# Each store of 128 finished tokens issued as two stores of 64 rows, one per batch (delta rule and gated feed-forward, one core)

## The chip, the core and the metric

The kernel runs on one core of one Trainium2 chip. The core has a matmul engine (TensorE; PE in the profile, its weight loads PEld), VectorE (DVE), ScalarE (ACT), GpSimd (POOL) and SyncE (SP), which here issues every transfer between memory (HBM) and the on-chip buffer (SBUF); the transfers themselves run on 16 DMA engines. The metric is the device time of one execution in microseconds (us), shorter being better. The kernel before took 704.14 us, the median of three runs (702.71 to 704.75).

## The reference

Two stages follow each other. The first is a delta rule over 768 time steps for 4 batches of 8 heads with head size 48; in each step the state of a head is read by the query and then corrected by the key:

```python
k_n = k / (np.linalg.norm(k, axis=-1, keepdims=True) + 1e-06)
for t in range(S):
    y[:, :, t] = np.einsum('bhd,bhde->bhe', q[:, :, t], state)
    v_old = np.einsum('bhde,bhd->bhe', state, kt)
    state = state + bt[:, :, :, None] * np.einsum('bhd,bhe->bhde', kt, vt - v_old)
```

The second is a feed-forward block on the 4 x 768 = 3072 tokens of 384 features that come out: `h = x @ w_in` (384 to 2048), `g = h * tanh(log1p(exp(h)))`, and `g @ w_out` (2048 to 384). The result has 3072 rows of 384 float32, ordered by batch and then by time.

## The kernel before, in words

Time is cut into 12 chunks of 64 steps. One unit `n` handles chunk `n` of all four batches, that is 256 tokens. The chunk form of the delta rule needs the products of a chunk's keys, transposed keys (`kt`, line 264) and a small triangular inverse that is built by a chain of VectorE instructions (`early`, lines 330 to 339); this is done for two chunks at a time, well ahead of their use. The keys for it come in by `load_src` (lines 176 to 183) into the buffers `ksrc`: eight loads per chunk, each of 32 rows, all issued by SyncE through `load` (line 171). The second set of eight follows in the same buffer once the first set has been transposed. Other loads of a unit bring queries (`qsrc`), keys (`xx`) and values (`vt`).

The feed-forward of a unit goes through 8 pairs of feature blocks: `g1` (line 561 on) makes `h` by 18 matmuls of line 575 and applies the nonlinearity on ScalarE and VectorE (lines 588 to 595); `g2` (line 600 on) adds to the two accumulators `acc[0]` and `acc[1]` by 12 matmuls of line 610. Each accumulator holds 128 tokens. Matmuls of the next units' delta rule are woven in between. After the last pair, `store(t)` copies accumulator `t` into an SBUF tile `o` with ScalarE (line 616) and SyncE issues the transfer to the output (line 618). There are 24 of these transfers: two for each of the 12 units. The two accumulators of the last unit are the last work of the kernel; behind them come only SyncE's wait for the transfers and the closing barrier (shown as line 815).

The 128 tokens of one accumulator are 64 time steps of batch `t` and the same 64 steps of batch `t + 2`. In the output these are two stretches of 64 consecutive rows, 1536 rows apart, so the target of line 618 is an access pattern of three dimensions: 2 batches, 64 rows, 384 features. Its source is the tile's 128 partitions with 384 features each.

The order on the engines: the generators put their steps at planned times into one heap (`put`, `defer`), which gives the order of the program; TensorE keeps that order from a planned time of 90 us on, while a scheduler that models the engines orders the instructions of the other engines, SyncE's transfers among them, as their inputs and buffers come free in its model. The order of the loads among themselves is held by line 173; the stores are not part of it. Each queue then runs strictly in order: a transfer whose wait is not over holds back what is behind it.

Of the kernel before, what the change touches and what calls it, by code (L numbers as in the profile page):

```python
# [35 lines left out]
def kernel(  # L36
# [22 lines left out]
    nc = tc.nc  # L59
# [18 lines left out]
    C = 64  # L78
# [37 lines left out]
    def tensor(dur):  # L116

        now[0] = max(now[0], tensor_free[0] if now[0] > TN['clk'] else 0.0)
        tensor_free[0] = now[0] + dur

    def defer(wait, f, *a):
        put(one(f, *a), now[0] + wait)
# [432 lines left out]
    def moe(n):  # L555

        NTT = UT // P
        acc = []
        gs = {}

        def g1(fp):
            end = n == NS - 1
            if end and fp % 3 in TN.get('hx', (2,)):
                h = pa.tile([P, 2, UT], F32, tag="at", name=f"h{n}_{fp}")
            else:
                h = ph.tile([P, 2, UT], F32, tag="h", name=f"h{n}_{fp}")
            xh, xl = xs[n]
            tensor(2.15)
            for f2 in range(2):
                f = 2 * fp + f2  # L570
                i = 0
                for c in range(NCH):
                    f0 = f * P % WI
                    for i2, x in ((0, xh), (0, xl), (1, xh)):
                        nc.tensor.matmul(h[:, f2, :], wt["i", f * P // WI * NCH + c][:, i2, f0:f0 + P], x[:, c, :],  # L575
                                         start=(i == 0), stop=(i == 3 * NCH - 1))
                        i += 1
            e = mp.tile([P, 2, UT], F32, tag="e", name=f"e{n}_{fp}")
            if end:

                gg = ap.tile([P, 2, 2, UT], F32R, tag="tn" if fp % 4 == 3 else "kt", name=f"g{n}_{fp}",
                             bufs=1 if fp % 4 == 3 else 3)
            else:
                gg = mp.tile([P, 2, 2, UT], F32R, tag="g", name=f"g{n}_{fp}", bufs=3)

            eng = nc.gpsimd if n in TN['pg'] else nc.vector
            t = 2.4
            for d, f in ((0.7, lambda: nc.scalar.activation(e, h, AF.Exp, scale=-1.0)),  # L588
                         (0.55, lambda: nc.vector.tensor_scalar(e, e, EXP20, 1.0, op0=ALU.min, op1=ALU.add)),  # L589
                         (0.65, lambda: nc.scalar.activation(e, e, AF.Square)),  # L590
                         (0.65, lambda: nc.scalar.activation(e, e, AF.Ln, bias=0.5, scale=0.5)),  # L591
                         (0.7, lambda: nc.scalar.activation(e, e, AF.Exp, scale=-1.0)),  # L592
                         (0.8, lambda: nc.vector.scalar_tensor_tensor(e, e, -1.0, h, op0=ALU.add, op1=ALU.mult)),  # L593
                         (0.7, lambda: nc.scalar.copy(out=gg[:, 0], in_=e)),  # L594
                         (0.8, lambda: eng.tensor_tensor(out=gg[:, 1], in0=e, in1=gg[:, 0], op=ALU.subtract))):  # L595
                defer(t, f)
                t += d
            gs[fp] = gg

        def g2(fp):  # L600
            gg = gs.pop(fp)
            tensor(2.1)
            if fp == 0:
                acc.extend(po.tile([P, 512], F32, tag=f"acc{t}", name=f"acc{t}_{n}")[:, :DM] for t in range(NTT))
            for t in range(NTT):
                ts_ = slice(t * P, (t + 1) * P)
                for f2 in range(2):
                    f = 2 * fp + f2
                    for i, (a, i2) in enumerate(((0, 0), (0, 1), (1, 0))):
                        nc.tensor.matmul(acc[t], gg[:, a, f2, ts_], wt["o", f][:, i2, :],  # L610
                                         start=(f == 0 and i == 0), stop=(f == NF - 1 and i == 2))

            if fp == NFP - 1:
                def store(t):
                    o = mp.tile([P, 512], F32, tag="w", name=f"o{n}_{t}")[:, :DM]
                    nc.scalar.mul(out=o, in_=acc[t], mul=-1.0)
                    dst = out.rearrange("(hh b r) f -> b hh r f", hh=2, b=2)[t, :, C * n:C * n + C, :]
                    nc.sync.dma_start(out=dst, in_=o)

                for t in range(NTT):  # L620
                    defer(1.3 * (t + 1), store, t)

        return g1, g2
# [196 lines left out]
```

## Time and profile before

| | us |
|---|---|
| median of 3 runs | 704.14 |
| the profiled execution, whole | 702.13 |
| its span, from the first to the last instruction | 700.3 |
| TensorE busy | 633.6 |
| VectorE busy | 478.4 |
| ScalarE busy | 440.0 |
| GpSimd busy | 48.8 |

The profiled execution is 2.0 us shorter than the median, and 1.8 us of it lie outside the span. The last matmul ends at 689.4 us, the last ScalarE instruction at 689.9 us and the span at 700.3 us. TensorE is busy for 90% of the span as a whole; it is below that mainly in the first quarter, where the weights are loaded and converted, and in a few places up to 242 us. The granted clock of TensorE over the span is 0.944 of full speed on average.

### The profile page before, as it was taken

What the parts mean: (1) busy time and instruction counts of PE and PEld (TensorE: products, weight loads), DVE (VectorE), ACT (ScalarE), POOL (GpSimd) and SP (SyncE); (2) the same over time, 40 slices, a digit from 0 to 9 for tenths busy, and PEclk for the clock granted to TensorE, in tenths of its full rate; (3) what the DMA queues carried; (4) which work ended last, traced back from release to release, by engine and by line L of the source; (5) the groups of instructions that cost most, each with busy time, mean ns of one, the idle gap of its engine ahead of it and who ended that gap; (6) DMA issues with size and microseconds to landing.
All of it is one profiled execution on the core that took longest, in us unless ns stands there. A gap on an engine that the chain in (4) does not pass through costs nothing.

```text
span 700.3 us, 23223 instructions
## 1 busy us (share of the span) xinstructions
PE 633.6 (90%) x10163; PEld 582.5 (83%) x10163; DVE 478.4 (68%) x1048; ACT 440.0 (63%) x821; POOL 48.8 (7%) x84
## 2 busy tenths in 40 slices
PE   6543899889979899999999999999999999999993
PEld 3313777679879799999999999999999999999993
DVE  4794278996449975589974799856899645443440
ACT  1350368776535766856758766668566687777771
POOL 5000000101000001010010000010100100000000
PEclk9575589999989999999999999999999999999998
DMA  5999230113131232222212312321121111000000
GB/s 81 223 244 348 40 61 12 22 15 59 27 63 26 42 59 39 41 52 35 46 37 42 63 25 39 66 37 30 31 35 47 28 21 36 13 22 3 12 12 24
DMA packets 160214, 37.79 MB, mean 54 GB/s; under 512 B 153456, under 2 KB 156528, under 8 KB 160112
## 3 DMA queue, kind: packets, MB, share of 16 engines
q1 hardware_dynamic: 160112, 36.30, 25.4%
q8 instruction: 80, 1.31, 0.7%
q14 instruction: 22, 0.18, 0.1%
HBM read 31.56 MB, written 4.72 MB: 52 GB/s over the span
## 4 chain that ended last, share of the span: by engine, by line
PE 44%; DVE 26%; ACT 13%; SPq 7%; issue 6%; DMA 3%; DVEq 0%; ACTq 0%
PE h L575 15%; PE acc L610 15%; SPq L171 7%; DVE e L593 4%; PE gq L433 3%; ACT e L591 3%; DVE g L595 3%; DVE pr L336 3%; DVE gt L338 3%; ACT e L590 2%; PE py L433 2%; ACT e L592 2%; DVE e L589 2%; DVE xx L480 2%; DVE xx L421 2%
## 5 line engine op out<-in xcount | busy, mean ns | idle before, releaser
L575 PE MATMUL h<-x,wi 128*128 128x256 f32 x1728 | 227.0, 285 | 4.3 <-DVE e L593 3.6
L575 PEld LDWEIGHTS h<-x,wi 128*128 128x128 f32 x1728 | 214.4, 188 | 10.5 <-DVE e L593 2.9
L610 PE MATMUL acc<-wo,g 128*128 128x384 f32 x1152 | 221.1, 341 | 0.0
L610 PEld LDWEIGHTS acc<-wo,g 128*128 128x128 f32 x1152 | 198.4, 188 | 3.2
L593 DVE SCALAR_TENSOR_TENSOR e<-e,h 128x512 f32<-128x512 f32 x96 | 65.8, 685 | 97.1 <-ACT e L592 93.8
L590 ACT ACTIVATE e<-e 128x512 f32<-128x512 f32 x96 | 60.6, 631 | 74.6 <-DVE e L589 74.1
L594 ACT CAST g<-e 128x512 fp32r<-128x512 f32 x96 | 59.5, 619 | 41.3 <-DVE e L593 40.8
L595 DVE TENSOR_TENSOR g<-e,g 128x512 fp32r<-128x512 f32 x96 | 65.1, 678 | 20.6 <-ACT g L594 19.4
L588 ACT ACTIVATE e<-h 128x512 f32<-128x512 f32 x96 | 57.1, 595 | 28.5 <-PE h L575 27.6
L591 ACT ACTIVATE e<-e 128x512 f32<-128x512 f32 x96 | 60.5, 631 | 2.6
L592 ACT ACTIVATE e<-e 128x512 f32<-128x512 f32 x96 | 60.6, 632 | 2.4
L589 DVE TENSOR_SCALAR e<-e 128x512 f32<-128x512 f32 x96 | 40.8, 425 | 25.1 <-ACT e L588 24.8
L338 DVE TENSOR_TENSOR gt<-gt,pr 128x84 f32<-128x84 f32 (+14 forms) x148 | 46.0, 311 | 3.2
L336 DVE TENSOR_TENSOR pr<-gt 128x84 f32<-128x84 f32 (+14 forms) x148 | 45.9, 310 | 2.5
L433 PE MATMUL gq<-xx,kt 64*64 64x112 f32 (+1 forms) x768 | 44.6, 264 | 0.9 <-ACT wo L243 0.9
L433 PEld LDWEIGHTS py<-xx 128*64 128x64 f32 x768 | 38.8, 142 | 6.3 <-issue 3.2
L480 DVE TENSOR_TENSOR xx<-gq,amask 64x256 f32<-64x256 f32 x96 | 40.2, 418 | 5.4 <-PE gq L433 4.7
L433 PE MATMUL py<-xx 128*64 128x48 f32 x768 | 42.8, 229 | 0.0
L433 PEld LDWEIGHTS gq<-xx,kt 64*64 64x64 f32 x768 | 38.2, 140 | 2.6 <-issue 1.3
L414 POOL TENSOR_TENSOR vt<-vt,ne 128x384 f32<-128x384 f32 x24 | 21.0, 880 | 277.8 <-DVE ne L328 123.3
L433 PE MATMUL pz<-vt,tt 64*64 64x48 f32 x768 | 38.0, 235 | 2.4 <-ACT tt L462 1.3
L433 PEld LDWEIGHTS pz<-vt,tt 64*64 64x64 f32 x768 | 34.4, 139 | 6.3 <-ACT tt L462 2.8
(112 smaller groups left out, 718.0 us busy)
## 6 DMA issues: line engine op xcount, KB each, us to landing
ri<-in_moe_w_in_dram SPq DMA_DIRECT2D x12, 512.0 KB
ro<-in_moe_w_out_dram SPq DMA_DIRECT2D x16, 384.0 KB
vt<-in_v_dram SPq DMA_DIRECT2D x48, 96.0 KB
xx<-in_k_dram SPq DMA_DIRECT2D x48, 96.0 KB
out_dram<-o SPq DMA_DIRECT2D x24, 192.0 KB
qsrc<-in_q_dram SPq DMA_DIRECT2D x48, 64.0 KB
ksrc<-in_k_dram SPq DMA_DIRECT2D x44, 64.0 KB
qsrc<-in_q_dram SPq DMA_DIRECT2D x48, 32.0 KB
```

What stands on the lines that cost most here:

```text
L336: nc.vector.tensor_tensor(out=pv, in0=nj, in1=xj, op=ALU.mult)
L338: nc.vector.tensor_tensor(out=below, in0=below, in1=pv, op=ALU.add)
L433: last[:] = [nc.tensor.matmul(*a, start=True, stop=True)]
L575: nc.tensor.matmul(h[:, f2, :], wt["i", f * P // WI * NCH + c][:, i2, f0:f0 + P], x[:, c, :], start=(i == 0), stop=(i == 3 * NCH - 1))
L588: for d, f in ((0.7, lambda: nc.scalar.activation(e, h, AF.Exp, scale=-1.0)), (0.55, lambda: nc.vector.tensor_scalar(e, e, EXP20, 1.0, op0 ...
L590: (0.65, lambda: nc.scalar.activation(e, e, AF.Square)),
L591: (0.65, lambda: nc.scalar.activation(e, e, AF.Ln, bias=0.5, scale=0.5)),
L592: (0.7, lambda: nc.scalar.activation(e, e, AF.Exp, scale=-1.0)),
L593: (0.8, lambda: nc.vector.scalar_tensor_tensor(e, e, -1.0, h, op0=ALU.add, op1=ALU.mult)),
L594: (0.7, lambda: nc.scalar.copy(out=gg[:, 0], in_=e)),
L595: (0.8, lambda: eng.tensor_tensor(out=gg[:, 1], in0=e, in1=gg[:, 0], op=ALU.subtract))):
L610: nc.tensor.matmul(acc[t], gg[:, a, f2, ts_], wt["o", f][:, i2, :], start=(f == 0 and i == 0), stop=(f == NF - 1 and i == 2))
```

## The change

Line 618 becomes a loop over the two batches of the accumulator. Each pass issues one transfer: 64 partitions of `o` to the 64 consecutive rows of that batch in the output. The bytes, the copy on ScalarE and the planned time of `store` are as before; SyncE issues 48 transfers to the output in place of 24.

```diff
                     nc.scalar.mul(out=o, in_=acc[t], mul=-1.0)
                     dst = out.rearrange("(hh b r) f -> b hh r f", hh=2, b=2)[t, :, C * n:C * n + C, :]
-                    nc.sync.dma_start(out=dst, in_=o)
+                    for hh in range(2):
+                        nc.sync.dma_start(out=dst[hh], in_=o[C * hh:C * hh + C])
```

## Rows read from the trace of the kernel before

**Rows 1.** The page, busy time of each engine over the span.
```profile
PE 633.6 (90%) x10163; PEld 582.5 (83%) x10163; DVE 478.4 (68%) x1048; ACT 440.0 (63%) x821; POOL 48.8 (7%) x84
```

**Rows 2.** Waits of TensorE from 242 us on: total, times, longest.
```profile
PE h L575 <- DVE e L593: 1.8, 4, 0.5
PE pz L433 <- ACT tt L462: 0.6, 3, 0.2
```

**Rows 3.** Chain of waits, 640 to 701 us: start, length, what.
```profile
681.00 8.39 PE acc L610 x48
...
689.41 0.49 ACT o L616
```

**Rows 4.** Timeline of SyncE's queue, last 13 us: start, length, what.
```profile
689.93 0.51 SPq L618 DMA_DIRECT2D out_dram<-o  x1
...
688.87 1.57 SPq L618 DMA_DIRECT2D out_dram<-o  x2
```

**Rows 5.** Waits of SyncE's queue in the last 13 us.
```profile
SPq L815 <- DMA out_dram<-o: 8.8, 1, 8.8
```

**Rows 6.** Instructions of line 815: durations min/median/max, first and last start.
```profile
L815 SPq EVENT_SEMAPHORE  x7: 17/28/28, 699.2 to 700.3; - x7
```

**Rows 7.** DMA view, 688 to 701 us, in 40 slices: GB/s.
```profile
GB/s 0 0 0 0 0 0 28 28 38 19 38 49 47 19 47 52 52 47 52 52 47 47 52 52 47 52 52 47 52 52 47 52 52 14 0 0 0 0 0 0
```

**Rows 8.** Windows: length, busy time of engines, granted clock, DMA share, GB/s.
```profile
690.40:698.80 8.40, 0.00 (x0) 0.00 (x0) 0.00 (x0) 0.00 (x0) 0.00 (x0) 0.68 0.13 46
...
208.20:209.30 1.10, 1.10 (x37) 0.97 (x37) 1.00 (x6) 1.08 (x3) 0.19 (x1) 1.00 0.72 132
```

**Rows 9.** The page, DMA issues: what, count, KB each.
```profile
out_dram<-o SPq DMA_DIRECT2D x24, 192.0 KB
```

**Rows 10.** Timeline of SyncE's queue, 188 to 212 us.
```profile
188.79 0.32 SPq L171 DMA_DIRECT2D ksrc<-in_k_dram  x1
189.21 0.65 SPq L618 DMA_DIRECT2D out_dram<-o  x1
189.91 6.79 SPq L171 DMA_DIRECT2D ksrc<-in_k_dram  x7
196.80 0.55 SPq L618 DMA_DIRECT2D out_dram<-o  x1
```

**Rows 11.** Chain of waits, 188 to 207 us.
```profile
196.21 2.10 DMA ksrc<-in_k_dram
...
198.48 1.26 DVE kt L264
```

**Rows 12.** Timeline of SyncE's queue: loads behind stores and without.
```profile
252.03 4.04 SPq L171 DMA_DIRECT2D xx<-in_k_dram  x2
...
272.23 1.28 SPq L171 DMA_DIRECT2D xx<-in_k_dram  x2
...
341.27 4.07 SPq L171 DMA_DIRECT2D ksrc<-in_k_dram  x8
```

**Rows 13.** Windows around the load's wait and behind it, columns as in rows 8.
```profile
198.50:205.40 6.90, 5.20 (x154) 4.82 (x156) 3.57 (x6) 1.12 (x3) 0.00 (x0) 0.51 0.43 69
205.40:242.00 36.60, 33.86 (x481) 32.17 (x478) 34.49 (x90) 22.50 (x42) 1.82 (x3) 1.00 0.21 32
```

**Rows 14.** Timeline of TensorE: start, length, what, [idle before, releaser].
```profile
192.14 1.99 PE L283 MATMUL pg<-kt 64*32 64x64 f32 x128
...
199.87 3.62 PE L283 MATMUL pg<-kt 64*32 64x64 f32 x125 [3.43 <-DVE kt L264]
...
236.79 2.40 PE L575 MATMUL h<-x,wi 128*128 128x256 f32 x18 [1.79 <-DVE e L593]
```

**Rows 15.** Timeline of VectorE, 196 to 207 us.
```profile
204.28 0.42 DVE L286 TENSOR_TENSOR d<-pg,lmask 128x256 f32<-128x256 f32 x1 [2.00 <-PE pg L283]
```

**Rows 16.** Waits of TensorE over the whole span.
```profile
PE ma L375 <- DVE tu L349: 13.5, 1, 13.5
```

## The prediction

> **What bounds the kernel now.** I read the page's busy times first. TensorE is busy 633.6 of 700.3 us [rows 1], so a change in another engine's queue counts only where TensorE waits for it, or after TensorE has finished. The waits of TensorE from 242 us on come next: 1.8 and 0.6 us in all [rows 2], so from there until its last matmul TensorE sets the time alone and takes nothing back that was won earlier. Third is the chain of waits at the end: matmuls until 689.39 us, the copy of the last accumulator from 689.41 for 0.49 us [rows 3], and then no engine works any more. The last store is issued at 689.93 [rows 4], SyncE waits 8.8 us for it [rows 5], the wait is over at 699.2, and the closing instructions run to 700.3 [rows 6]. So about 9.3 us between 689.9 and 699.2 belong to the stores alone. The DMA view shows what they do there: bytes flow from slice 7 (689.95 us) to slice 34 (it ends at 699.05), at about 50 GB/s [rows 7]. The window over the same stretch gives a DMA share of 0.13 at 46 GB/s [rows 8]. 0.13 of 16 is 2.1 engines: two engines carry two stores of 192 KB [rows 9], and 14 stand idle. Compare the load of `xx`, 64 rows per transfer, where the share is 0.72 [rows 8]: at least 11 engines. The store's target has 2 batches as its outermost dimension, the load has 64 rows, and two is the number of engines that the store gets. The last place to look is the other one with stores ahead of a wait of TensorE: 188 to 206 us [rows 10, 11, 14].
>
> **The change part by part.**
>
> *The last four transfers (the tail).* Each new store has 64 rows outermost on both sides, as the `xx` load has, so I take it to be spread over 16 engines. SyncE now issues four in place of two. One issue takes 0.51 to 0.65 us [rows 4, 10]; I take 0.55 with 0.04 between two. The first pair goes out from 688.87 [rows 4] to 690.01, which is after the copy that the second pair waits for, so the third starts at 690.05 and the fourth at 690.64; the last issue is 0.7 us later than now. From the start of the first issue (688.87) to the first bytes it now takes 1.1 to 1.4 us (slice 7 starts at 689.95 [rows 7]); I take 1.2, giving 691.84. Per engine the stores now move 46 / 2.1 = 22 GB/s [rows 8]; 98 KB over 16 such engines take 98 / 352 = 0.28 us, and the three transfers ahead, 0.59 us apart, are through by then: 692.1. From the last bytes to the end of the wait it is now 0.15 to 0.47 us (slice 34 is 698.73 to 699.05, the wait ends at 699.2); 0.4 gives 692.5. The closing 1.1 us [rows 6] give 693.6 in place of 700.3: 6.7 us less. With every short end of these (lag 1.1, no data time, 0.15) it is 7.3 less; with issues of 0.65 and half of the engines, about 6.0; if the engines stay two, 0.7 more than now.
>
> *The two stores of unit 0 (189 to 206 us).* Seven loads of keys stand behind the first store. They take 6.79 us to issue, 0.97 each [rows 10], while eight such loads with no store just ahead take 4.07, 0.51 each [rows 12]. The same is seen at 252 us: two `xx` loads behind a pair of stores take 4.04 us, and 1.28 where none is ahead [rows 12]. So SyncE is held up while two engines work off a store: the loads also need those two. The last of the seven is handed over at 196.21 and lands 2.10 us later, and only then does `kt` start at 198.48 [rows 11] and TensorE at 199.87, after 3.43 us of waiting [rows 14]. After the change: the first store's halves end at 189.86 + 0.59 = 190.45, seven loads by 0.51 end at 194.1, landing 2.1 later at 196.2, `kt` at 196.4. That is 2.1 us earlier, and TensorE's wait becomes 1.3 us. The second effect is the clock. It is granted 0.51, the 1.2 GHz level, from 198.5 to 205.4 us [rows 13], after that wait; 125 matmuls of `pg` take 3.62 us there, 128 of them took 1.99 at 192 us [rows 14]. A wait of 1.79 us at 236.79 [rows 14] left the clock at 1.00, the 2.4 GHz level, through 242 us [rows 13]. So with 1.3 us I expect no fall, and `pg` gains another 1.6. VectorE's last step on `pg` had waited 2.00 us for it at 204.28 [rows 15] and starts its chain 3.7 earlier. From 205.4 to 242 TensorE is busy 33.86 of 36.60 us [rows 13], and its longest wait there is for VectorE, whose chain moves along; so I carry 3.5 us through. Bounds: the full wait and the `pg` slowdown gone give 3.4 + 1.6 = 5.0 less; the two extra issues in front of the loads, 2 x 0.6, with nothing won give 1.2 more. 3.5 is nearest to the rows of loads that have no store ahead, which is what the loads will see.
>
> *The other 20 stores.* Each adds an issue of 0.55 us on SyncE, and the loads behind a pair get back 4.04 - 1.28 = 2.8 against it. What hides either is that the loads come well before use: after 242 us no load is among TensorE's waits [rows 2]. I count 0. Without that cover it would be 0.55 each for what is late, less the 2.8 per pair. The tiles `o` are needed again a whole unit later, so their release decides nothing.
>
> *A rule that speaks against.* The row on two engines is [rows 8]. Against it stands the Trainium skill, page "DMA: Bandwidth & Descriptors", section "Rules for kernel authors": two transfers to disjoint halves of the partitions gain nothing, because both spread over all 16 engines and so serialize; one transfer of 128 partitions is better. By that rule the tail would lose 0.7 us, and it is a rival below. The same page, section "Why a DMA increments its semaphore by 16 and not by 1", says that the number of engines is the largest up to 16 that divides the slowest dimension of both access patterns: 2 for the store now, 16 for a half. The trace agrees with the 2; no run so far shows a store on 16.
>
> **The sum.** Against the profiled execution: 702.13 - 6.7 - 3.5 + 0 = 691.9 us. The median of the runs, 704.14, is 2.0 above that execution, so the forecast for the median is 693.9.
>
> **The rivals.**
>
> *Only the tail.* The loads of `ksrc` are issued faster, but the 188 to 242 us stretch gives nothing, because VectorE or ScalarE instructions stand in another order there or another wait takes the place. For it: VectorE's chain is close to gapless after 205 us (34.49 of 36.60 busy [rows 13]). Against: that chain starts behind `pg`. 702.13 - 6.7 + 2.0 = 697.4.
>
> *The halves are not spread.* The rule above, or a transfer that is cut in some other way, leaves the data time as it is: four issues, the same 8 us of bytes. For it: no store of this trace runs on more than two engines. Against: the `xx` load with 64 rows [rows 8]. 704.14 + 0.7 = 704.8, or 706.0 if the extra issues at 189 us count too.
>
> *The order of the other engines turns.* The order on VectorE, ScalarE and SyncE is planned by modelled times, TensorE's is fixed. 24 more transfers shift that plan from 189 us on, and one VectorE step put behind a chain makes TensorE stand still. The price of one such wait in this trace: `ma` waited 13.5 us for `tu` [rows 16]. With the stretch's gain lost that gives 704.14 - 6.7 + 13.5 = 710.9: slower. It decides once new waits exceed the 6.7 us of the tail. For it: nothing in the program holds the order of VectorE. Against: the stores write only the output, so no VectorE instruction depends on one; after 242 us the waits are 2.4 us in all, so there is slack for small shifts.
>
> **How the numbers follow.** Forecast 0.55, only the tail 0.27, not spread 0.06, order turned 0.06; the other 0.06 are smaller stalls that leave 699 to 704. The forecast's own range, from the bounds of both terms (6.0 to 7.3, and 2.0 to 5.0), is 691.8 to 696.1. Tail alone reaches 697 to 698. The range 691.5 to 699.0 holds both. A run of this kernel can be told from no change beyond about 0.3%, 2.1 us. Faster by more: 0.55 + 0.27 and most of the smaller stalls, 0.88. Within: not spread and the rest of these, 0.07. Slower: 0.05.
>
> **What would show it.** Right: in the tail a DMA share far above 0.13 in short bursts from about 690 us, four issues on SyncE, a wait of line 815 of about 2 us in place of 8.8, and a span that ends some 4 us after the last copy. At 190 us: seven loads in about 4 us, `kt` near 196.4, a wait of `pg` near 1.3 us, no half clock behind it. Wrong: a share still near 0.13 (the first step fails and the time is unchanged), a `pg` wait above 3 us or the half clock still there (697), or a new long wait of TensorE for VectorE after 206 us (slower).

## The result, and the profile after

The changed kernel takes 696.68 us, the median of six runs (694.38 to 697.96), against 704.22 for the kernel before beside it: a ratio of 0.9895, 95% interval 0.9876 to 0.9913, or 7.4 us less by that ratio. Faster was forecast, and the time lies in the range given (691.5 to 699.0). It is not the 693.9 of the likeliest case; it stands 0.7 us from the rival "only the tail" (697.4).

The profiled execution took 696.11 us with a span of 694.4. First the tail, row by row. The timeline of ScalarE gives the last two copies (start, length, what):

```profile
688.77 0.49 ACT L616 ACTIVATE o<-acc 128x384 f32<-128x384 f32 x1 [2.90 <-PE acc L610]
689.83 0.49 ACT L616 ACTIVATE o<-acc 128x384 f32<-128x384 f32 x1 [0.56 <-PE acc L610]
```

SyncE's queue issues four stores where it issued two [rows 4]:

```profile
689.29 2.39 SPq L619 DMA_DIRECT2D out_dram<-o  x4
```

Its wait for the stores, in total, times and longest, is 1.6 us in place of 8.8 [rows 5]:

```profile
SPq L816 <- DMA out_dram<-o: 1.6, 1, 1.6
```

And the closing instructions (old line 815 is now 816) start at 693.3, not 699.2 [rows 6]:

```profile
L816 SPq EVENT_SEMAPHORE  x7: 17/28/28, 693.3 to 694.3; - x7
```

So from the end of the last copy (689.83 + 0.49 = 690.32) to the end of the span it is now 4.1 us; it was 700.3 - 689.90 = 10.4. The tail gave 6.3 us. The DMA view of the last 5.5 us (busy tenths and GB/s in 40 slices) shows why; the row of before is [rows 7]:

```profile
DMA  0000000000589417992299614995000000000000
GB/s 0 0 0 0 0 0 0 0 0 0 145 201 246 112 45 201 223 201 56 67 246 201 168 34 134 212 235 123 11 0 0 0 0 0 0 0 0 0 0 0
```

Four bursts at up to nine tenths of the 16 engines and 246 GB/s, with gaps between: the engines now wait for SyncE's next issue, where two engines were busy without a gap at about 50 GB/s.

Then the stretch of unit 0's stores, which was to give the rest. SyncE's queue, to set beside [rows 10]:

```profile
189.58 0.32 SPq L171 DMA_DIRECT2D ksrc<-in_k_dram  x1
189.99 1.18 SPq L619 DMA_DIRECT2D out_dram<-o  x2
191.23 4.89 SPq L171 DMA_DIRECT2D ksrc<-in_k_dram  x7
196.21 1.98 SPq L619 DMA_DIRECT2D out_dram<-o  x2
...
251.24 3.26 SPq L619 DMA_DIRECT2D out_dram<-o  x4
254.60 1.35 SPq L171 DMA_DIRECT2D xx<-in_k_dram  x2
```

The seven loads behind the first store take 4.89 us in place of 6.79, and the two `xx` loads behind a pair of stores at 254 us 1.35 in place of 4.04 [rows 12]. But four issues took 3.26 us there where two had taken 1.21 before, so most of it is spent again. The row of before:

```profile
250.73 1.21 SPq L618 DMA_DIRECT2D out_dram<-o  x2
```

What happens on the other side of these loads is in the chain of waits (start, length, what):

```profile
191.85 1.60 SPq L171
...
195.63 2.79 DMA ksrc<-in_k_dram
198.41 0.45 issue
...
199.05 1.25 DVE kt L264
...
200.44 1.98 PE pg L283 x125
202.42 2.14 issue
204.56 0.31 PE pg L283 x3
```

One load took 1.60 us to issue. `kt` started at 199.05, and the 125 `pg` matmuls ran in 1.98 us, at full clock as forecast. Then TensorE stood for 2.14 us ("issue": it waits for nothing that the profile shows) ahead of the last three. From the start of `pg` to those three it is 4.12 us; before it was 3.95 (from 199.87 [rows 14] to the row below).

```profile
203.82 0.42 PE L283 MATMUL pg<-kt 64*32 64x64 f32 x3 [0.33 <-issue]
```

The half clock came all the same, only later, as the windows show (columns as in [rows 8]):

```profile
198.50:202.50 4.00, 2.49 (x127) 2.04 (x127) 2.58 (x4) 1.34 (x4) 0.00 (x0) 1.00 0.33 55
202.50:205.30 2.80, 0.74 (x21) 0.64 (x22) 0.40 (x1) 0.00 (x0) 0.00 (x0) 1.00 0.51 64
205.30:208.80 3.50, 3.50 (x60) 3.41 (x55) 2.74 (x6) 1.47 (x5) 0.00 (x0) 0.51 0.06 8
```

From 242 us on TensorE's waits are those of before to the tenth (1.8 and 0.6 us, [rows 2]). The order of the instructions on VectorE, ScalarE and GpSimd is the same in both programs; on SyncE, two pairs of stores that had a key load between them now stand together.

### The profile page after: what moved, and what is told of

Its sections match the earlier page's. It is cut to its first block, busy times and chain, and to the rows that moved or that the text cites. A ratio compares the mean times of both kernels' runs of the same rounds, so it can differ in the third digit from the quotient of the medians.

```text
span 694.4 us, 23260 instructions
## 1 busy us (share of the span) xinstructions
PE 636.3 (92%) x10163; PEld 584.6 (84%) x10163; DVE 478.3 (69%) x1048; ACT 440.0 (63%) x821; POOL 48.8 (7%) x84
## 4 chain that ended last, share of the span: by engine, by line
PE 45%; DVE 25%; ACT 13%; issue 6%; SPq 6%; DMA 3%; POOL 0%; DVEq 0%; ACTq 0%; POOLq 0%
PE h L575 16%; PE acc L610 15%; SPq L171 6%; DVE e L593 4%; PE gq L433 3%; ACT e L591 3%; DVE g L595 3%; DVE pr L336 3%; DVE gt L338 2%; ACT e L590 2%; ACT e L592 2%; PE py L433 2%; DVE e L589 2%; DVE xx L421 2%; DVE xx L480 2%
```

## The experiments

The kernel before ran beside each on the same chip (medians 703.95 to 704.95); "split" is the changed kernel.

**Which stores matter.** Two kernels, each with one half of the change: halves in the last unit alone, or everywhere else. The edit is against the kernel before.

```diff
-                    nc.sync.dma_start(out=dst, in_=o)
+                    if n == NS - 1:          # the other kernel: n < NS - 1
+                        for hh in range(2):
+                            nc.sync.dma_start(out=dst[hh], in_=o[C * hh:C * hh + C])
+                    else:
+                        nc.sync.dma_start(out=dst, in_=o)
```

> Only the two accumulators of the last unit go out in halves; the other 22 stores are whole, as before. Theory A (all of the gain is the tail: the last stores run on 16 engines in place of 2): the wait for the stores at the end is about 1.6 us in place of 8.8, the span ends about 4.1 us after the last copy in place of 10.4, and the time is 697 to 698.5 (ratio to the kernel before 0.989 to 0.992), the same as the full change within 0.3%. Theory B (part of the gain comes from the 22 stores amid the loads): the time is 2 us or more above that of the full change, 699 or more.

Measured: 698.09 us, ratio 0.9918 (0.9887 to 0.9949); from the last copy to the end 4.3 us.

> The 22 stores before the last unit go out in halves; the last two are whole. Theory A: the tail is as before (a wait of 8.8 us, 10.4 us from the last copy to the end), and the time is that of the kernel before within 0.3% (702.5 to 706). Theory B: 2 to 4 us faster than before (700 to 702).

Measured: 704.05 us, ratio 0.9993 (0.9974 to 1.0012); the tail is 10.4 us as before, its window shows two engines, and SyncE waits as long as in [rows 5]:

```profile
696.00:705.00 9.00, 0.00 (x0) 0.00 (x0) 0.00 (x0) 0.01 (x1) 0.00 (x0) 0.73 0.13 44
```

```profile
SPq L819 <- DMA out_dram<-o: 8.7, 1, 8.7
```

Theory A holds: 5.8 us (3.6 to 8.0) come with four transfers out of 48, and the other 44 give 0.5 us, with an interval of 0.8 lost to 1.8 gained. The two halves are not told apart more finely than that.

**Two transfers, or more engines.** The same number of transfers, cut along the columns, so that both still have the two batches in front.

```diff
-                    for hh in range(2):
-                        nc.sync.dma_start(out=dst[hh], in_=o[C * hh:C * hh + C])
+                    for c in range(2):
+                        s = slice(c * DM // 2, (c + 1) * DM // 2)
+                        nc.sync.dma_start(out=dst[:, :, s], in_=o[:, s])
```

> Each store goes out as two transfers again, but cut by columns: both batches and 192 of the 384 columns each, so the outermost dimension of the target stays 2. Theory A (what counts is the number of engines, set by the 2 batches in front): DMA share in the tail stays about 0.13, the wait at the end is 9 us or more, the time is that of the kernel before or up to 3 us above it (704 to 707; rows of 768 bytes may move at a lower rate). Rival (it helps to have two smaller transfers in flight in place of one): the wait at the end falls to 5 us or less, the time is 701 or less.

Measured: 705.06 us, ratio 1.0008 (0.9988 to 1.0027). The window of its tail (copy ends at 692.39):

```profile
693.00:700.00 7.00, 0.00 (x0) 0.00 (x0) 0.00 (x0) 0.00 (x0) 0.00 (x0) 0.74 0.14 44
```

The share is 0.14, the bytes move at 44 GB/s, and copy to end is 10.6 us. SyncE's last wait is 6.2 us and not the 9 expected, because its four issues themselves took 4.32 us: it was held while the engines worked. Two smaller transfers are worth nothing as such.

**Rows that divide by two or by sixteen.** In the last unit the 64 rows of a batch go out as 62 and 2, or as 32 and 32: eight transfers each, into the same contiguous stretches.

```diff
                     for hh in range(2):
-                        nc.sync.dma_start(out=dst[hh], in_=o[C * hh:C * hh + C])
+                        if n < NS - 1:
+                            nc.sync.dma_start(out=dst[hh], in_=o[C * hh:C * hh + C])
+                        else:
+                            for r0, r1 in ((0, 62), (62, 64)):      # the other kernel: (0, 32), (32, 64)
+                                nc.sync.dma_start(out=dst[hh, r0:r1], in_=o[C * hh + r0:C * hh + r1])
```

> The full change, but in the last unit each batch's 64 rows go out as 62 and 2 rows: eight transfers in place of four. Theory A (a transfer is spread over as many engines as divide its rows, up to 16; 62 and 2 give two engines): the DMA share of the tail is about 0.13 again, it takes about 10 us or more from the last copy to the end in place of 4.1, and the time is 703 to 706. Rival (a transfer into one contiguous stretch of the output is spread over all 16 whatever its rows): the tail is that of four issues more, 4.1 + 4 x 0.59 = 6.5 us, and the time about 699.

> The full change, but in the last unit each batch's 64 rows go out as 32 and 32: eight transfers, as in the kernel with 62 and 2 rows. Theory A (32 rows also go to 16 engines, and the tail is now paced by the issues on SyncE, 0.59 us each): 6.0 to 6.5 us from the last copy to the end, time 698.5 to 699.5. Rival (the bytes still pace the tail): the four extra issues run beside the bytes and the time is that of the full change, 696.7 within 0.7.

Measured: 62 and 2 rows 703.36 us, ratio 0.9989 (0.9968 to 1.0010), 10.4 us from the last copy to the end; 32 and 32 rows 698.34, ratio 0.9908 (0.9878 to 0.9937), 4.6 us. One window of each tail, 62 and 2 first:

```profile
694.00:700.00 6.00, 0.00 (x0) 0.00 (x0) 0.00 (x0) 0.00 (x0) 0.00 (x0) 0.74 0.13 46
```

```profile
689.00:692.50 3.50, 0.00 (x0) 0.00 (x0) 0.00 (x0) 0.09 (x1) 0.00 (x0) 1.00 0.42 107
```

A share of 0.13 against 0.42 with the same number of transfers into the same places. That is the cause of the tail's gain, shown: the number of rows in front decides how many engines carry a transfer. For the 32-row kernel the tail lies between the two expectations: the four extra issues cost 0.5 us, not 2. All eight together took 3.60 us (0.45 each, not 0.59), so that they end 2.6 us after the last copy against 1.4, and the wait behind the last was 0.8 us against 1.6.

**What is left of the tail.** The last of the four transfers goes out from ScalarE.

```diff
                     for hh in range(2):
-                        nc.sync.dma_start(out=dst[hh], in_=o[C * hh:C * hh + C])
+                        eng = nc.scalar if (n, t, hh) == (NS - 1, NTT - 1, 1) else nc.sync
+                        eng.dma_start(out=dst[hh], in_=o[C * hh:C * hh + C])
```

> The full change, and the very last of the four transfers of the tail is issued by ScalarE, which has nothing left to do, beside SyncE's third. Theory A (the tail is paced by the issues): 3.5 us from the last copy to the end in place of 4.1, time 695.8 to 696.2 (0.6 below the full change). Rival (landing of the last bytes and the closing set it, not the issues): 4.1 us, the same time.

Measured: 695.46 us, ratio 0.9872 (0.9844 to 0.9900). In its profile the last copy ends at 694.53 and the span at 698.1, a tail of 3.6 us as expected: SyncE's three and ScalarE's one go out side by side.

```profile
693.50 1.75 SPq L620 DMA_DIRECT2D out_dram<-o  x3
694.04 0.49 ACT L616 ACTIVATE o<-acc 128x384 f32<-128x384 f32 x1 [0.56 <-PE acc L610]
694.56 0.57 ACTq L620 DMA_DIRECT2D out_dram<-o  x1
```

The time lies below the 695.8 to 696.2 expected and below the split kernel's, with overlapping intervals; the 0.5 us of the tail are seen in the profile, not proved by the times.

**Why the stretch gave nothing: the loads.** Unit 0's stores are planned 8 us later, behind the key loads.

```diff
-                    for hh in range(2):
-                        nc.sync.dma_start(out=dst[hh], in_=o[C * hh:C * hh + C])
+                    def send():
+                        for hh in range(2):
+                            nc.sync.dma_start(out=dst[hh], in_=o[C * hh:C * hh + C])
+
+                    if n == 0:
+                        defer(8.0, send)
+                    else:
+                        send()
```

> The full change, and the stores of the first unit are planned 8 us later, so that SyncE issues them behind the second set of eight key loads rather than ahead of seven of them. Theory L (the stores ahead of these loads hold up kt, as the prediction had it): the loads are issued in about 4 us, TensorE's wait for kt (1.4 us in the changed kernel, 3.4 before) goes, pg takes 2.0 us without a pause, and the time is 2.5 to 3.5 us below the full change (about 693.5). Theory C (the pg stretch is paced by TensorE's own instruction loads: 4.0 to 4.1 us from its start to its last matmuls in both kernels so far, at either clock): the wait for kt goes, but the pause of about 2 us inside pg stays, and the time is 0 to 1.5 us below the full change (695 to 696.7).

Measured: 696.60 us, ratio 0.9882 (0.9858 to 0.9907): as the split kernel. The eight loads are issued in 4.69 us and are out at 195.64, yet `kt` starts at 198.82. The chain of waits gives the last load 3.50 us from its issue:

```profile
190.95 4.69 SPq L171 DMA_DIRECT2D ksrc<-in_k_dram  x8
```

```profile
195.15 3.50 DMA ksrc<-in_k_dram
198.65 0.17 issue
198.82 1.25 DVE kt L264
```

VectorE's timeline shows that `kt` could not have come much earlier (last column: idle before, and releaser); the row of `kt` before stands behind it:

```profile
197.63 0.69 DVE L593 SCALAR_TENSOR_TENSOR e<-e,h 128x512 f32<-128x512 f32 x1 [3.09 <-ACT e L592]
198.24 0.42 DVE L286 TENSOR_TENSOR d<-pg,lmask 128x256 f32<-128x256 f32 x1
198.82 1.25 DVE L264 STREAM_TRANSPOSE kt<-ksrc 128x1024 f32<-128x1024 f32 x1 [0.17 <-issue]
```

```profile
198.48 1.25 DVE L264 STREAM_TRANSPOSE kt<-ksrc 128x1024 f32<-128x1024 f32 x1 [2.20 <-DMA ksrc<-in_k_dram]
```

Ahead of `kt` in VectorE's order stand the gating step of line 593, which waits 3.09 us for ScalarE, and the step on the previous `pg`, which ends at 198.66, as the last load comes in. In the split kernel the same two rows end at 198.41, 0.64 us before `kt`. So the loads can win at most the 2.2 us that VectorE had waited for them before. TensorE's wait for `kt` was still 1.0 us, and 1.1 us in the kernel with both edits, further down, whose loads were in well before; theory L is refuted for the time. Theory C's rows are there: `pg` starts at 200.21, stops, and its last three come at 203.78, 3.57 us later, though no half clock was granted anywhere near:

```profile
200.21 1.98 PE pg L283 x125
202.19 1.59 issue
203.78 0.31 PE pg L283 x3
```

**The pause inside `pg`.** The second half of `pg` is planned behind the next delta-rule and `h` matmuls, and the VectorE chain on it 2.5 us later.

```diff
-              ..., g2=(-3.2,-2.75,-2.7,-2.69,-2.67,-2.64,-2.631), ...
+              ..., g2=(-3.2,-2.75,-2.7,-2.69,-2.67,-2.64,-2.585), ...
-                                                *spread(-2.6, TN['sg'], 30 if g < FG else 63), -1.43)))
+                                                *spread(-2.55 if g == 2 else -2.6, TN['sg'], 30 if g < FG else 63), -1.43)))
```

> The full change, and on TensorE the second half of the pg matmuls behind the wait for kt in unit 1's time is moved behind the next delta-rule and h matmuls, with VectorE's chain on them planned about 2.5 us later. Theory C (TensorE is paced there by its own instruction loads, 4 us for a stretch of small matmuls): the pause shows up at another place, again 3.9 us or more from the start of pg to the matmuls of the next block of instructions or in the pauses marked issue, and the time gains less than 1 us (696 to 698). Rival (pg's pause is a wait for the accumulator buffers that VectorE frees): pg's first half runs through without a pause, py and ps follow at once, and the time falls by 1.5 to 2 us (695).

Measured: 696.49 us, ratio 0.9875 (0.9852 to 0.9897), not to be told from the split kernel. All of TensorE's waits between 185 and 245 us:

```profile
PE pg L283 <- DVE kt L264: 4.0, 1, 4.0
PE pz L433 <- issue: 1.2, 1, 1.2
```

The pause is gone, and so are the waits for line 593; but in this execution the loads came late, `kt` cost 4.0 us, and the half clock was granted behind that wait:

```profile
201.00:207.00 6.00, 5.01 (x128) 4.78 (x128) 2.23 (x5) 0.75 (x3) 0.00 (x0) 0.50 0.36 44
```

At the half clock the pause had been 0.33 us in the kernel before too, so this profile does not show that the move took it away. Inconclusive on the time: what the pause had cost was not seen to come back.

**Both edits, and the split kernel again on one chip.** The two edits above (ScalarE's transfer and the later stores) together, and the changed kernel unchanged.

> Two edits together on top of the full change: the last transfer of the tail goes out from ScalarE, and the first unit's stores are planned behind the key loads. If the two add as the profiles of the single edits say (tail 3.6 us in place of 4.1; no wait of kt for a load, but pg paced at 3.6 to 4.1 us as before), the time is 0.5 to 1.0 us below the full change on the same chip (about 695.5). Rival (the loads ahead do matter for the time, and the single run missed it): 1.5 us or more below the full change.

Measured: 695.61 us, ratio 0.9880 (0.9852 to 0.9908); tail 3.6 us. The six times stand in two groups, three from 692.8 to 693.7 and three from 697.5 to 698.1. In its profile the key loads were issued without a store ahead of them and landed 2.6 to 3.6 us after issue, where the trace has the landing, and `kt` stood behind VectorE's own queue alone:

```profile
189.54 4.04 SPq L171 DMA_DIRECT2D ksrc<-in_k_dram  x8
```

```profile
DMA to landing us min/median/max: 2.6/2.9/3.6
```

```profile
199.75 0.42 DVE L286 TENSOR_TENSOR d<-pg,lmask 128x256 f32<-128x256 f32 x1
200.09 1.24 DVE L264 STREAM_TRANSPOSE kt<-ksrc 128x1024 f32<-128x1024 f32 x1
```

> The changed kernel itself, on the same chip as the kernel above, as a second sample of it: the ratio to the kernel before of 0.9895 comes again within 0.2% (697 for 704.3), the tail of 4.1 us from the last copy to the end too. What is asked of the profile is the wait for kt at 190 to 205 us: if splitting the stores had taken it down for good, it is 1.4 us again; if it hangs on the run, it may lie anywhere between 1 and 4 us while the time stays.

Measured: 697.89 us, ratio 0.9902 (0.9878 to 0.9927), so the result repeats; tail 4.1 us. The wait for `kt` is 2.3 us, and the half clock stands at yet another place. Here the row that matters is `pg`, 3.95 us from its start to its last three again, with part of it at the half clock:

```profile
200.94 3.33 PE L283 MATMUL pg<-kt 64*32 64x64 f32 x125 [2.34 <-DVE kt L264]
204.89 0.30 PE L283 MATMUL pg<-kt 64*32 64x64 f32 x3 [0.62 <-issue]
```

Against the split kernel beside it the two edits are 2.3 us faster in the medians (695.61 against 697.89), which is the rival's difference, while 695.6 is the time of the first expectation; the intervals overlap, so neither is shown. They and the ScalarE transfer alone (695.46) have the lowest medians of all; neither is proved faster than the split kernel.

## Why the prediction was right, and where it was not

**Two engines, then more than fourteen: right.** The share of 0.13 was read as two engines, and the cause as the 2 in front. The kernels with 62 and 2 rows and with columns keep 0.13 and 0.14 and the old time; 64 and 32 rows do not. The Trainium skill, page "DMA: Bandwidth & Descriptors", section "Why a DMA increments its semaphore by 16 and not by 1", says the largest number up to 16 that divides the slowest dimension of both sides; the traces agree at 2, 62 and the pair in front (0.13 to 0.14), and the share rises to 0.9 in single slices for 64 rows, more than 14 engines, and to 0.8 for 32 rows, more than 12. The rule against halves on that page of the Trainium skill ("Rules for kernel authors") did not decide here: it presupposes that the whole transfer already runs on all 16, and this one did not.

**The tail: right to 0.4 us.** Forecast 6.7 us less, measured 6.3 in the profiled execution (10.4 to 4.1). The single terms: the fourth issue ended at 689.29 + 2.39 = 691.68, 1.36 us after the last copy; the wait for the last bytes was 1.6 us, and the closing 1.1. That the issues on SyncE set what is left was also right: taking one of them off it gave 3.6.

**The stretch at 189 to 206 us: the mechanism was there, the term was 3.5 us and is about 0.5.** This is the step that failed: "I carry 3.5 us through". The 44 transfers outside the last unit give 0.5 us, 0.8 lost to 1.8 gained. Part by part:
- "Seven loads by 0.51": they took 4.48 to 5.45 us in the split kernels, not 3.57, and the two halves ahead of them 1.18 to 2.43 us. In each execution one or two of these nine issues take 1.1 to 2.1 us. TensorE's wait for `kt` was accordingly 1.1 to 4.0 us in the kernels that split unit 0's stores ahead of the loads (seven profiles: 1.4, 3.0, 2.8, 1.1, 4.0, 1.3, 2.3), against 3.4 and 3.7 with whole stores: less on average, and down to the 1.3 of the forecast in three of the seven.
- `kt` has a second bound that I did not look for: VectorE's own queue, which is held by line 593 and by the step on the `pg` before. In four profiles (loads ahead, both edits, ScalarE's transfer, 32 rows) `kt` starts within 0.2 us of the end of that step, and TensorE's wait is then 1.0 to 1.3 us. The forecast's 2.1 us stayed just inside this bound; earlier loads can win no more.
- "`pg` gains another 1.6": it does run in 1.98 us at full clock, and then TensorE stands for 1.6 to 2.1 us. From its start to its last three matmuls it is 3.95 us before and 3.57 to 4.12 in ten other profiles, whatever the clock. So within `pg` the half clock had cost next to nothing. In all these eleven a load on the queue for instructions (16 KB, about 1 us) starts 1.1 to 1.9 us into `pg`, and the last three matmuls follow 2.2 to 2.6 us after its start, which makes the fetching of TensorE's own instructions the likely cause; it is inferred, not shown. The Trainium skill, page "Runtime: NRT & Kernel Launch", section "Instruction fetch mechanics", says that an engine fetches the next block of 256 instructions while it runs the current one and that crossing a border is mostly hidden; 125 matmuls and as many weight loads are nearly such a block, and if the pause is that crossing, it shows here as 1.6 to 2.1 us.
- "I carry 3.5 us through": where the loads went ahead, the stretch itself did win 3.0 us. From the start of the first `pg` matmuls to the first `h` matmul behind the stretch it is 11.3 us in both such profiles, against 14.3 and 14.5 with whole stores. But to the copy of unit 1's first accumulator, 40 us on, it is 53.2 in both, against 54.3 and 54.5: 1.0 to 1.3 us are left. One row shows where 1.5 us went with the loads ahead:

```profile
236.57 3.91 PE L575 MATMUL h<-x,wi 128*128 128x256 f32 x18 [1.80 <-DVE e L593]
```

The same matmuls behind the same wait took 2.40 us before [rows 14]; here they ran mostly at the half clock (0.57 granted from 236.5 to 240.5 us). In six split kernels the time to that copy is 52.1 to 55.7 us, so a single profile shows a win of 2 us or a loss of 1; from the copy on, the eleven profiles without the moved `pg` take the same 443.4 to 443.6 us to the end of the last copy.

The half clock did not go either. In the split kernel it was granted later, at 205.3 us; across the profiles it comes at different places between 170 and 245 us. Behind the shortest waits for `kt` (1.0 and 1.1 us, three profiles) there is none, but these three have it some 42 to 48 us after the first `pg`, where before had none. That a shorter wait would prevent it was argued from one row of before, the `h` matmuls behind 1.79 us, and the row above has the same wait with the half clock.

**The other 20 stores: right.** 0 was forecast, and the waits of TensorE after 242 us did not change. The expected balance (2.8 us back per pair of stores against 1.2) is 2.7 back against 2.05 spent: the issues of this burst of four were dearer (0.82 each on average) than the 0.59 taken.

**The rivals.** "Only the tail" had 0.27 and is what happened, in part for the reason it named: another wait takes the place. "Not spread" is refuted by the tail of every kernel whose last transfers have 64 or 32 rows. "The order turns" did not come up: the order on the three compute engines is unchanged, and no wait after 206 us is new. The range held since it reached over both cases. The likeliest case was chosen too high: its second term rested on loads far from any store and on one row for the clock, and the next bound behind each was not checked. Its range for that term, 2.0 to 5.0, has no row for the 2.0 and leaves out the bound that its own section had named, nothing won and 1.2 us lost; the measured 0.5 lies between.

## What to carry to other kernels

In the tail of a kernel read the DMA share of the transfers, times 16: a number like 2 points to a small outermost dimension. Splitting the access pattern so that 64 rows stood in front was worth 6.3 us here, and each extra issue cost 0.45 to 0.6. The same fault in the middle of the kernel cost nothing that these runs could tell from noise, since another engine set the time there. Before a gain in a stretch is carried through, look for the next bound of each step: the instruction ahead of it in its own queue, a pause that a slower clock may have covered, and a clock that may fall later instead.

## What was not expected of the hardware

- TensorE's block of 125 small matmuls and their weight loads took 3.57 to 4.12 us up to the next matmul at 2.4 GHz and at 1.2 GHz alike, with a pause of 0.33 us where all of it ran at the half clock and 1.6 to 2.1 us where all ran at the full one.
- A transfer that runs on two engines holds up the queue that issues behind it: two loads take 4.04 us, and 1.35 behind the same bytes sent as halves. Among the issues of the split kernels single ones still took over 1 us, like the 1.60 at 191.85 above. In the nine profiles that split unit 0's stores by rows, SyncE has 195 such issues after 100 us, and every one of them overlaps a load on one of the two queues for instructions; of its 2214 shorter issues 381 do. That the two go together is shown, what holds the issue is not. The DMA view from 191.70 to 193.45 us of the changed kernel has one:

```profile
q8 instruction: 1, 0.02, 4.7%
```

- The end of the last copy lies between 689.1 and 696.0 us across twelve profiles of kernels that differ little before it, and the clock differs between them in places where the instructions are the same. Differences of 1 to 2 us between two single profiles say nothing; the lengths of short stretches within them say more.
